# Attention and an ELU network on one core: the next block's operands made at other places of the order, and the weights' sums begun a block earlier

## The chip, the core and the metric

The kernel runs on one core of a Trainium2 chip. The time is the device's, in microseconds (us), of one execution. TensorE (PE) multiplies matrices into PSUM, VectorE (DVE) and ScalarE (ACT) work on PSUM and SBUF, GpSimd (POOL) on SBUF; SyncE (SP) issues all the DMAs of this kernel, in its own order. An engine takes its instructions in order and waits at the first whose inputs or buffer aren't ready.

## The reference

```python
scores = scale * np.matmul(q_c, k_c.transpose(0, 1, 2, 4, 3))   # chunks of 64 positions
scores = scores - np.max(scores, axis=-1, keepdims=True)
attn = np.exp(scores)
attn = attn / (np.sum(attn, axis=-1, keepdims=True) + 1e-09)
out = np.matmul(attn, v_c)
...
x = np.ascontiguousarray(attn_out.transpose(0, 2, 1, 3)).reshape(B * S, H * D)   # 4608 x 512
h = x @ w_in                                                    # 512 -> 2048
g = np.where(h > 0.0, h, alpha * (np.exp(np.minimum(h, 0.0)) - 1.0))
return (g @ w_out).astype(np.float32)                           # 2048 -> 512
```

Batch, heads, positions and head size are 8, 8, 576 and 64. The weights come as doubles (two 32-bit words each).

## The kernel before

A float32 factor is kept as a high part (rounded to the format fp32r) and a low part (the rest), and a product is three matmuls (`three`, L406): high by high, high by low, low by high.

The 4608 rows of x are done in nine blocks of 512, each of four tiles of 128 rows. A tile's attention runs beside the products of the block before: loads of q, k and v; 32x32 transposes on DVE (L283 for q, L286 for k into `k_apart`); scores on PE (L357); softmax (L363 and L377 on DVE, the exponent L381 on ACT, L383 to L385 and the scaling L316 on DVE); eight small DMAs that move rows (y<-y, L328) and a transpose into `a_apart` (L333); the product with v (L341); and a copy into `xf` (L392 on ACT). `k_apart` and `a_apart` exist once, so tiles follow each other in turn.

Blocks 0 and 1 are plain: 16 steps f, each with a product h = x w_in of 128 columns (`hidden`), the ELU (Relu and exponent on ACT L423 and L424, a DVE step L426, a high part ghi on ACT L431, a low part glo on DVE L434), and the product with w_out (`project`). In block 0 the weights are also split into high and low parts (units of `split_units`; L160 is a low part).

Blocks 2 to 8 work in pairs of steps, by Strassen's scheme with seven products of half size instead of eight. Products p1 to p7 need sums of weight quarters (A11 to S4) and of x's quarters (B11, B21, B22 and T1 to T4). p2, p5 and p3 go to one PSUM buffer (y), the rest to another (x). ACT keeps what is in x by copies (c1 to c4, L613), DVE adds y and a kept part (d1 to d3, L618). The results are the halves A (straight) and B (cross) of the pair; each passes through an ELU (L622 and L623 on ACT, L625 on DVE, the high part L630 on ACT, the low part L632 on POOL), and their products with w_out (Q, one per tile of rows) fill PE between the next pair's products.

The weights' sums are made in block 1 by `combine`: for each of eight pairs six operations on POOL (L481, 512 and 256 wide), a copy of 1024 elements to the high part on ACT (L506), the subtract for the low part on POOL (L481, 1024 wide), and DMAs to `a_dram` (L498, L499 for the weights' own parts, L511 for the sums). From there four DMAs for each pair (`load_operands`, L530) bring the operands back, three pairs' places in turn. x's operands are made by `prepare_x` at the end of each block from block 1: differences t1 to t4 on DVE (L554), and for each operand a high part on ACT and a low part on POOL (L558, L559).

PE, ACT, DVE and SP run in the order in which the program is written. That order is set by strings: one item is one step of a generator. H is `hidden`, e a part of an ELU, P a plain step's `project`, a and n steps of the current and the next attention tile, L the next tile's loads, x a step of `prepare_x`, w one load of operands, A and B parts of the two ELUs. LAST_STEP is the last step of block 1, FIRST_PAIR the first pair of block 2, LAST_PAIR a block's last pair. POOL gets its order from the order in which the program names its work.

## Time and profile before

| | |
|---|---|
| median of 3 runs | 908.12 us (906.46 to 908.53) |
| profiled execution | 905.94 us, its span 904.1 us |
| PE busy | 874.0 us (97%) |
| DVE, ACT, POOL busy | 537.4, 497.3, 285.4 us |
| PE clock granted | 0.996 of full |
| DMA | 195.05 MB, 216 GB/s on average |

The span is the time that the records of the profile cover. Block 0 runs up to about 134 us of it, block 1 to about 240, and each of the seven later blocks takes some 94.7 us. "A <- B" in a row is an output and its inputs; in brackets at the end stands how long the engine idled before it and what ended that. Operands of the weights and of the paired ELU's results lie in the memory of the plain weights, so their names read `wi_hi`, `wi_lo`; `h` is PSUM of the first product, `o` of the second, and `t` are the differences.

### The profile page before, as it was taken

How to read it: one execution, taken by the hardware profiler on the slowest of the kernel's cores; microseconds unless marked ns; L12 is line 12 of the kernel's file. 1: busy time of each engine (PE TensorE's matmuls, PEld its weight loads, DVE VectorE, ACT ScalarE, POOL GpSimd, SP SyncE). 2: the span in 40 equal slices, each digit the busy share in tenths (PEclk: the TensorE clock that was granted, in tenths of full speed). 3: DMA queues.
4: the chain of work that ended last, by engine and by line, in shares of the span. 5: the costliest groups of instructions: out<-in, count | busy, mean ns of one | idle time of the engine just before them, and what ended most of it. 6: DMA issues, size and time to landing. Idle time of an engine off the chain costs nothing.

```text
span 904.1 us, 15897 instructions
## 1 busy us (share of the span) xinstructions
PE 874.0 (97%) x5870; PEld 752.6 (83%) x5870; DVE 537.4 (59%) x833; ACT 497.3 (55%) x966; POOL 285.4 (32%) x229
## 2 busy tenths in 40 slices
PE   7899999998989999999999999999999999999998
PEld 6688877876788888888888888887888788889896
DVE  5899888564755576556655665557555755442222
ACT  6899974443444455444644464455444554464443
POOL 2000025677322243224422252226222622253222
PEclk9999999999999999999999999999999999999999
DMA  8785444769887768777679859776768597466421
GB/s 204 214 264 183 161 117 157 241 211 311 248 227 234 240 217 281 233 232 227 202 240 271 253 198 279 227 218 194 260 207 267 166 304 212 177 228 229 166 83 46
DMA packets 161309, 195.05 MB, mean 216 GB/s; under 512 B 67536, under 2 KB 123856, under 8 KB 161232
## 3 DMA queue, kind: packets, MB, share of 16 engines
q1 hardware_dynamic: 161232, 194.04, 68.6%
q8 instruction: 46, 0.75, 0.4%
q14 instruction: 31, 0.25, 0.1%
HBM read 162.53 MB, written 24.12 MB: 206 GB/s over the span
## 4 chain that ended last, share of the span: by engine, by line
PE 73%; DVE 7%; ACT 5%; issue 4%; DMA 4%; POOL 3%; SPq 3%; POOLq 0%; ACTq 0%; DVEq 0%
PE o L406 34%; PE h L406 32%; PE ps_a L357 3%; PE ps_a L341 2%; POOL st L481 2%; DMA wi_hi<-a_dram 1%; DVE t L554 1%; DVE y L316 1%; DMA q_sb<-in_q_dram 1%; SPq L247 1%; POOL wi_lo L632 1%; ACT wi_hi L630 1%; DMA wi_lo<-a_dram 1%; DVE z L383 1%; PE ps_a L265 1%
## 5 line engine op out<-in xcount | busy, mean ns | idle before, releaser
L632 POOL TENSOR_TENSOR wi_lo<-e,wi_hi 128x512 fp32r<-128x512 f32 x112 | 144.9, 1294 | 418.2 <-ACT wi_hi L630 418.2
L613 ACT COPY kept<-h 128x256 f32<-128x256 f32 x224 | 82.1, 367 | 189.8 <-PE h L406 189.7
L618 DVE TENSOR_TENSOR kept<-h,kept 128x256 f32<-128x256 f32 x168 | 70.9, 422 | 191.9 <-PE h L406 133.1
L406 PE MATMUL h<-xhi,wi_hi 128*128 128x256 f32 (+1 forms) x720 | 182.5, 305 | 1.9 <-ACT xhi L558 1.3
L406 PE MATMUL o<-wo_lo,wi_hi 128*128 128x512 f32 x448 | 177.6, 397 | 0.0
L406 PE MATMUL o<-wo_hi,wi_hi 128*128 128x512 f32 x448 | 177.4, 396 | 0.0
L406 PE MATMUL o<-wo_hi,wi_lo 128*128 128x512 f32 x448 | 175.2, 391 | 2.0 <-POOL wi_lo L632 1.6
L406 PEld LDWEIGHTS h<-xhi,wi_hi 128*128 128x128 f32 x720 | 125.3, 189 | 19.7 <-issue 3.2
L406 PE MATMUL h<-xlo,wi_hi 128*128 128x256 f32 (+1 forms) x424 | 133.7, 315 | 2.0 <-DVE xlo L399 1.1
L406 PE MATMUL h<-xhi,wi_lo 128*128 128x256 f32 (+1 forms) x432 | 118.1, 318 | 0.4 <-DVE kept L618 0.4
L406 PEld LDWEIGHTS h<-wi_lo,wi_hi 128*128 128x128 f32 x666 | 94.0, 189 | 14.8 <-ACT kept L613 3.6
L406 PEld LDWEIGHTS o<-wo_hi,wi_lo 128*128 128x128 f32 x448 | 84.2, 188 | 23.8 <-POOL wi_lo L632 5.2
L625 DVE SCALAR_TENSOR_TENSOR e<-e,kept 128x512 f32<-128x512 f32 x112 | 77.3, 690 | 43.5 <-ACT e L623 39.9
L622 ACT ACTIVATE e<-kept 128x512 f32<-128x512 f32 x112 | 70.8, 632 | 55.8 <-DVE kept L618 53.6
L406 PE MATMUL h<-wi_lo,wi_hi 128*128 128x256 f32 x666 | 97.8, 282 | 3.4 <-ACT kept L613 1.7
L630 ACT CAST wi_hi<-e 128x512 fp32r<-128x512 f32 x112 | 69.7, 623 | 47.0 <-DVE e L625 46.6
L406 PEld LDWEIGHTS h<-xlo,wi_hi 128*128 128x128 f32 x424 | 80.0, 189 | 12.7 <-DVE xlo L399 1.8
L406 PEld LDWEIGHTS o<-wo_lo,wi_hi 128*128 128x128 f32 x448 | 85.6, 191 | 2.6
L406 PEld LDWEIGHTS o<-wo_hi,wi_hi 128*128 128x128 f32 x448 | 84.6, 189 | 2.9
L406 PEld LDWEIGHTS h<-xhi,wi_lo 128*128 128x128 f32 x432 | 76.4, 189 | 11.8 <-DVE kept L618 1.6
L623 ACT ACTIVATE e<-e 128x512 f32<-128x512 f32 x112 | 70.8, 632 | 3.6
L481 POOL TENSOR_TENSOR st<-wi_hi,wi_lo 128x512 f32<-128x512 f32 x16 | 22.3, 1418 | 133.0 <-DMA st<-in_k_dram 121.2
(90 smaller groups left out, 1362.0 us busy)
## 6 DMA issues: line engine op xcount, KB each, us to landing
wi_hi<-a_dram SPq DMA_DIRECT2D x148, 448.0 KB, 5.5
wi_lo<-a_dram SPq DMA_DIRECT2D x76, 448.0 KB, 5.3
kept<-in_q_dram SPq DMA_DIRECT2D x80, 128.0 KB, 7.9
kept<-in_k_dram SPq DMA_DIRECT2D x80, 128.0 KB, 5.7
st<-in_moe_w_in_dram SPq DMA_DIRECT2D x16, 512.0 KB, 4.2
st<-in_moe_w_out_dram SPq DMA_DIRECT2D x16, 512.0 KB, 4.7
a_dram<-st SPq DMA_DIRECT2D x16, 512.0 KB, 5.2
y<-y SPq DMA_DIRECT2D x224, 32.0 KB, 1.9
```

What stands on the lines that cost most here:

```text
L247: nc.sync.dma_start(out=qk[p0:p0 + n // U, w0:w0 + NK * U * D].rearrange("p (h w) -> p h w", h=NK), in_=src[b, j::2, s0:s0 + n, :].rearran ...
L341: nc.tensor.matmul(x_ps[j * D:(j + 1) * D, hp, :], lhsT=v_sb[:, h, :], rhs=a_apart[:, h, :], start=True, stop=True,)
L357: nc.tensor.matmul(s_ps[cs, 2 * hp:2 * hp + 2, :], lhsT=qT[:, hp, cs], rhs=kbd[:, hp, :, cs], start=True, stop=True,)
L406: nc.tensor.matmul(ps, lhsT=a, rhs=b, start=start, stop=stop, skip_group_check=onto)
L481: nc.gpsimd.tensor_tensor(out=out, in0=a, in1=b, op=op)
L613: nc.scalar.copy(out=out, in_=self.x)
L618: nc.vector.tensor_tensor(out=out, in0=self.y, in1=self.kept[kept], op=ALU.add)
L622: nc.scalar.activation(out=e, in_=c, func=AF.Relu, scale=-1.0)
L623: nc.scalar.activation(out=e, in_=e, func=AF.Exp, scale=-1.0)
L625: nc.vector.scalar_tensor_tensor(out=e, in0=e, scalar=-1.0, in1=c, op0=ALU.add, op1=ALU.max)
L630: nc.scalar.copy(out=ghi, in_=e)
L632: nc.gpsimd.tensor_tensor(out=glo, in0=e, in1=ghi.bitcast(F32), op=ALU.subtract)
```

## The change

1. **x's operands.** In the order strings the x steps stand at other places, and `prepare_x` goes B11, B21, then the differences t1, t2, t4, then T2, the difference t3, T1, T3, T4, B22 (before: B11, differences, B21, T2, T1, t3 with T3, T4, B22). t1 and t3 take buffers of the plain ELU (`ghi`, `glo` of the pool gp), which the first copies of outputs use too, in place of `y` and `q_sb`. In FIRST_PAIR the projections (Q) stand at other places as well.
2. **The weights' sums.** The three buffers `kept_st` are made at the end of block 0. Sums take the second and third in turn. Those of pairs 0 and 1 are called for in block 0 (f=14 and 15). The low part's subtract moves from POOL to DVE. The stores of the weights' own parts are divided (high or low).
3. **q and k in a buffer of their own.** The tiles of block 1 and the first of the next put q and k all in `kept_st[0]`, each after the one before has been transposed; the last unit of weights is staged in `a_apart`, which is set to zero only afterwards, at the end of block 0.
4. **Loads.** `load_operands` becomes one generator over all pairs; in block 1 two loads of the second pair come earlier than before, and PAIRS has one w more.
5. The last pair's low parts are made on DVE instead of POOL.

The three places at which the prediction rests, in the order of one engine. All line numbers of the changed kernel are shifted (L554 is now L569, L618 L634, L625 L641, L632 L649, L559 L574).

DVE at a block's last pair, the first one, before; `t` are the differences, the two kinds of `kept` the additions d and the ELU's STT:

```order
L618 TENSOR_TENSOR kept<-h,kept 128x256
L554 TENSOR_TENSOR t<-xf 128x512
L554 TENSOR_TENSOR t<-xf,t 128x512 x2
L618 TENSOR_TENSOR kept<-h,kept 128x256
L625 SCALAR_TENSOR_TENSOR e<-e,kept 128x512
L363 TENSOR_REDUCE mx<-ps_a 128x8
L377 TENSOR_TENSOR a<-ps_a,mx 128x512
L383 TENSOR_REDUCE z<-a 128x8
```

And with the change:

```order
L641 SCALAR_TENSOR_TENSOR e<-e,kept 128x512
L367 TENSOR_REDUCE mx<-ps_a 128x8
L381 TENSOR_TENSOR a<-ps_a,mx 128x512
L569 TENSOR_TENSOR t<-xf 128x512
L569 TENSOR_TENSOR t<-xf,t 128x512 x2
L634 TENSOR_TENSOR kept<-h,kept 128x256
L387 TENSOR_REDUCE z<-a 128x8
```

The three differences went from ahead of d1 to behind the first half of the softmax, just ahead of d2.

DVE at the end of block 1 (LAST_STEP) and in the first pair, before; L426 and L434 are the last plain ELU:

```order
L363 TENSOR_REDUCE mx<-ps_a 128x8
L377 TENSOR_TENSOR a<-ps_a,mx 128x512
L554 TENSOR_TENSOR t<-xf 128x512
L554 TENSOR_TENSOR t<-xf,t 128x512 x2
L426 SCALAR_TENSOR_TENSOR e<-e,h 128x512
L434 TENSOR_TENSOR glo<-e,ghi 128x512
L618 TENSOR_TENSOR kept<-h,kept 128x256
L383 TENSOR_REDUCE z<-a 128x8
```

And with the change:

```order
L381 TENSOR_TENSOR a<-ps_a,mx 128x512
L387 TENSOR_REDUCE z<-a 128x8
L388 TENSOR_SCALAR z<-z 128x8
L389 RECIPROCAL z<-z 128x8
L320 TENSOR_TENSOR y<-a,z 128x8x2x32
L569 TENSOR_TENSOR t<-xf 128x512
L569 TENSOR_TENSOR t<-xf,t 128x512 x2
L569 TENSOR_TENSOR t<-xf 128x512
L430 SCALAR_TENSOR_TENSOR e<-e,h 128x512
L438 TENSOR_TENSOR glo<-e,ghi 128x512
```

The rest of the softmax with the scaling, and t3, now stand ahead of the last plain ELU.

SP at the beginning of block 1, before; `st` takes q and k of a tile, in two buffers in turn:

```order
L247 DMA st<-in_q_dram 32x4x256 x4
L247 DMA st<-in_k_dram 32x4x256 x4
L219 DMA v_sb<-in_v_dram 128x8x64
L455 DMA out_dram<-k_sb 128x512
```

And with the change, from the second tile's loads (into the buffer that the first tile's are read from):

```order
L251 DMA kept<-in_q_dram 32x4x256 x4
L251 DMA kept<-in_k_dram 32x4x256 x4
L223 DMA v_sb<-in_v_dram 128x8x64
L459 DMA out_dram<-k_sb 128x512
L459 DMA out_dram<-q_sb 128x512
L459 DMA out_dram<-k_sb 128x512
L459 DMA out_dram<-q_sb 128x512
L519 DMA a_dram<-kept 128x1024 x2
L332 DMA y<-y 32x256 x8
```

The store of the first sums (L519) and the first y moves stand behind loads that wait for the tokens' one buffer.

```diff
@@ -112,8 +112,12 @@
-        st = stp.tile([P, STAGE], U32, name="st")[:, :2 * 4 * P * 2].rearrange(
-            "p (i a b t) -> p i a b t", i=2, a=4, t=2)
+        if u < NF:
+            st = stp.tile([P, STAGE], U32, name="st")[:, :2 * 4 * P * 2]
+        else:
+            st = a_apart.rearrange("p h t -> p (h t)").bitcast(U32)
+        st = st.rearrange("p (i a b t) -> p i a b t", a=4, b=P, t=2)
@@ -480,10 +484,12 @@
+        def place_of(g):
+            return kept_st[1 + g % 2][:, :2 * 8 * P].rearrange("p (l a f) -> p l a f", l=2, f=P)
         def sums(g):
-            st = stp.tile([P, STAGE], F32R, name="st")[:, :2 * 8 * P].rearrange(
-                "p (l a f) -> p l a f", l=2, f=P)
-            w, s = st[:, 0].bitcast(F32), st[:, 1].bitcast(F32)
+            st = place_of(g)
+            w, s = st[:, 0], st[:, 1]
             for i in range(2):
@@ -493,42 +499,51 @@
-            for lo in range(2):
-                w1, w2 = w_in_slices(2 * g)[lo], w_in_slices(2 * g + 1)[lo]
-                nc.sync.dma_start(out=rows(g, lo)[:, :4], in_=w1.bitcast(F32))
-                nc.sync.dma_start(out=rows(g, lo)[:, 4:6], in_=w2[:, 2:].bitcast(F32))
-            return st
...
-        def split(g, st):
-            nc.scalar.copy(out=st[:, 0], in_=st[:, 1].bitcast(F32))
-            pool(st[:, 1], st[:, 1].bitcast(F32), st[:, 0].bitcast(F32), ALU.subtract)
-        def write(g, st):
+        def write_parts(g, lo):
+            w1, w2 = w_in_slices(2 * g)[lo], w_in_slices(2 * g + 1)[lo]
+            nc.sync.dma_start(out=rows(g, lo)[:, :4], in_=w1.bitcast(F32))
+            nc.sync.dma_start(out=rows(g, lo)[:, 4:6], in_=w2[:, 2:].bitcast(F32))
+        def split(g):
+            st = place_of(g)
+            nc.scalar.copy(out=st[:, 0].bitcast(F32R), in_=st[:, 1])
+            nc.vector.tensor_tensor(
+                out=st[:, 1].bitcast(F32R), in0=st[:, 1], in1=st[:, 0], op=ALU.subtract)
+        def write_sums(g):
             for lo in range(2):
-                nc.sync.dma_start(out=rows(g, lo)[:, 6:], in_=st[:, lo].bitcast(F32))
-        made = {}
-        for third in range(3 * NG + 6):
-            g, part = divmod(third, 3)
-            if part == 0 and g < NG:
-                made[g] = sums(g)
-            elif part == 2 and g < NG:
-                split(g, made[g])
-            elif part == 1 and 0 <= g - 1 < NG:
-                write(g - 1, made[g - 1])
-            yield
...
+                nc.sync.dma_start(out=rows(g, lo)[:, 6:], in_=place_of(g)[:, lo])
+        for step in range(-2, NF):
+            for g in range(NG):
+                since = step - (2 * g - 3 if g > 1 else g - 2)
+                if since == 0:
+                    sums(g)
+                    write_parts(g, 0)
+                if since == 1:
+                    split(g)
+                if since == 1 + g % 2:
+                    write_parts(g, 1)
+                if since == 2:
+                    write_sums(g)
+            yield
+    def load_operands():
+        for g in range((NB - PLAIN) * NG):
+            buf, src = place(g % 3), a_dram[g % NG]
+            for i in range(4):
+                part = slice(i * HALF // 2, (i + 1) * HALF // 2)
+                while g > pairs_begun + 1:
+                    yield
+                nc.sync.dma_start(out=buf[:, part].bitcast(F32), in_=src[:, part])
+                yield
@@ -563,19 +578,20 @@
         split("B11", b11, nc.gpsimd)
         yield
-        t1, t2, t4 = t_tile(wst, "y"), t_tile(io, "q_sb"), t_tile(io, "q_sb")
+        split("B21", b21, nc.gpsimd)
+        yield
+        t1, t2, t4 = t_tile(gp, "ghi"), t_tile(io, "q_sb"), t_tile(io, "q_sb")
         minus(t1, b12, b11)
         minus(t2, b22, t1)
         minus(t4, b21, t2)
         yield
-        split("B21", b21, nc.gpsimd)
-        yield
         split("T2", t2, nc.gpsimd)
         yield
+        t3 = t_tile(gp, "glo")
+        minus(t3, b22, b12)
+        yield
         split("T1", t1, nc.gpsimd)
         yield
-        t3 = t_tile(io, "q_sb")
-        minus(t3, b22, b12)
         split("T3", t3, nc.gpsimd)
         yield
         split("T4", t4, nc.gpsimd)
@@ -629,7 +645,8 @@
             ghi, glo = g_places(which)
             nc.scalar.copy(out=ghi, in_=e)
             yield
-            nc.gpsimd.tensor_tensor(out=glo, in0=e, in1=ghi.bitcast(F32), op=ALU.subtract)
+            engine = nc.vector if self.g == (NB - PLAIN) * NG - 1 else nc.gpsimd
+            engine.tensor_tensor(out=glo, in0=e, in1=ghi.bitcast(F32), op=ALU.subtract)
@@ -698,17 +715,18 @@
     PAIRS = (
-        "p1 c1 Q p2 d1 w x B Q x p6 c2 B Q B p5 w n n Q p7 c3 d2 A w a Q Q p4 c4 A w Q p3 d3 A A Q B",
-        "n a a L p1 c1 Q p2 d1 w B Q p6 c2 B Q B n n p5 w Q n p7 c3 d2 A n Q Q p4 c4 A w Q p3 d3 A A "
+        "p1 c1 x Q p2 d1 w B Q p6 c2 B x Q B p5 w x n n Q p7 c3 d2 A w a Q Q p4 c4 A w Q p3 d3 A A "
+        "Q B",
+        "n a a L p1 c1 Q p2 d1 w B Q p6 c2 B Q B n n p5 w Q n p7 c3 d2 A w n Q Q p4 c4 A w Q p3 d3 A A "
         "Q B w",
     )
     LAST_PAIR = (
-        "n a a L p1 c1 x x Q p2 d1 w B Q B x p6 c2 B Q n n x p5 w x Q n p7 c3 d2 A n Q Q p4 c4 x A w "
-        "Q p3 d3 A A Q B w"
+        "n a a L p1 c1 x Q p2 d1 w B Q p6 c2 B Q B x n p5 w x n Q p7 c3 d2 A n Q Q p4 x c4 A w x n Q "
+        "p3 d3 A A x Q B w"
     )
-    LAST_STEP = "n a a n H n x x x P e x e e x e"
+    LAST_STEP = "n a a n H n x x n x P n e x x e e x e"
     FIRST_PAIR = (
-        "p1 c1 p2 d1 w a a Q p6 c2 Q x p5 w x n n Q p7 c3 d2 w A Q a x p4 c4 A w p3 d3 A A B"
+        "p1 c1 x p2 d1 w Q Q x p6 c2 w Q p5 x w p7 c3 Q d2 n n A w p4 c4 A w a p3 d3 A A B"
     )
@@ -773,8 +791,15 @@
-    loads, combining, preparing, pair, kept_st = {}, combine(), iter(()), None, []
+    combining, loading, pairs_begun = combine(), load_operands(), 0
+    preparing, pair, kept_st = iter(()), None, []
...
+    def plain_loads(f: int):
+        for _ in range({LOADED + 1: 1, LOADED + 2: 2, LOADED + 3: 1, NF - 1: 2}.get(f, 0)):
+            next(loading)
+        next(combining, None)
@@ -785,16 +810,17 @@
+    def place_of_tokens(n: int):
+        return kept_st[1 if n % 2 and n > (PLAIN + 1) * NTT else 0]
     def later_loads(n: int):
-        qk = kept_st[n % 2] if kept_st else stp.tile([P, STAGE], F32, name="st")
-        return load_tokens(n * P, qk), load_heads(v, "v_sb", n * P, io)
+        return load_tokens(n * P, place_of_tokens(n)), load_heads(v, "v_sb", n * P, io)
...
     nc.gpsimd.memset(k_apart, 0.0)
-    nc.gpsimd.memset(a_apart, 0.0)
@@ -822,6 +848,10 @@
                     if item == "H":
                         if blk == 0:
                             split_upto(f)
+                            if f == NF - 2:
+                                kept_st += [stp.tile([P, STAGE], F32, name="kept", tag="st")
+                                            for _ in range(3)]
+                                sums = kept_st[2]
                             if f == NF - 1:
                                 loaded = later_loads(2 * NTT)
@@ -848,24 +878,21 @@
+                if blk == PLAIN - 2 and f >= NF - 2:
+                    next(combining)
+                if (blk, f) == (0, NF - 1):
+                    split_upto(NU - 1)
+                    nc.gpsimd.memset(a_apart, 0.0)
                 if blk == PLAIN - 1:
-                    for _ in range(2):
-                        next(combining, None)
-                    if f == NF - 2:
-                        kept_st += [
-                            stp.tile([P, STAGE], F32, name="kept", tag="st") for _ in range(3)]
-                        sums = kept_st[2]
-                        upcoming = later_tile(n + 1, *later_loads(n + 1))
-                    if f >= LOADED:
-                        i = f - LOADED
-                        if i % 4 == 0:
-                            loads[i // 4] = load_operands(i // 4)
-                        next(loads[i // 4])
+                    plain_loads(f)
+                if (blk, f) == (PLAIN - 1, NF - 4):
+                    loaded = load_tokens((n + 1) * P, place_of_tokens(n + 1))
+                if (blk, f) == (PLAIN - 1, NF - 2):
+                    upcoming = later_tile(n + 1, loaded, load_heads(v, "v_sb", (n + 1) * P, io))
...
                 g = (blk - PLAIN) * NG + f // 2
...
-                if g + 2 < (NB - PLAIN) * NG:
-                    loads[g + 2] = load_operands(g + 2)
+                pairs_begun = g + 1
@@ -907,7 +934,7 @@
                     elif item == "w":
-                        next(loads.get(g + 2, iter(())), None)
+                        next(loading, None)
```

7 lines of the change are left out of this document (1 added, 6 removed).

## The prediction

> **What bounds the kernel now.** I read the page first, then busy times by stretch, PE's waits, and the timelines of the places that the change touches.
>
> ```profile
> PE 874.0 (97%) x5870; PEld 752.6 (83%) x5870; DVE 537.4 (59%) x833; ACT 497.3 (55%) x966; POOL 285.4 (32%) x229
> PE 73%; DVE 7%; ACT 5%; issue 4%; DMA 4%; POOL 3%; SPq 3%; POOLq 0%; ACTq 0%; DVEq 0%
> ```
>
> PE is busy for 97% of the span and holds 73% of the chain. The change adds and removes no matmul (in the first pair some only trade places), so what can move are PE's stalls, some 30 us of 904.1. The stretches tell where they lie (length, then PE, PEld, DVE, ACT and POOL busy, PE's clock, DMA):
>
> ```profile
> 135.00:165.00 30.00, 28.27 (x156) 22.81 (x157) 23.40 (x34) 11.70 (x19) 16.32 (x14) 1.00 0.56 192
> 195.00:225.00 30.00, 25.64 (x131) 19.54 (x130) 15.68 (x21) 10.78 (x17) 19.75 (x16) 1.00 0.87 284
> 245.00:257.00 12.00, 8.42 (x62) 7.11 (x63) 6.16 (x9) 6.14 (x13) 5.07 (x4) 0.86 0.78 264
> 395.24:418.41 23.17, 23.17 (x168) 20.65 (x166) 12.48 (x21) 11.21 (x23) 5.18 (x5) 1.00 0.77 227
> 418.41:443.55 25.14, 24.26 (x168) 20.27 (x166) 18.48 (x26) 14.88 (x31) 14.81 (x12) 1.00 0.61 169
> ```
>
> The last two rows run from one tile's value product (L341) to the next. With the same 168 matmuls the one inside a block takes 23.17 and the one over a block boundary 25.14: a stall of 1.97 where POOL works 14.81 instead of 5.18. Five boundaries have such a tile behind them. Block 1 shows 1.73 and 4.36 of idle PE in the first two rows, the handover to the paired work 3.58 in the third.
>
> **Part 1, the end of block 0.** The sums of the first two weight pairs start on POOL when the buffer each takes is free: after the last read of its staging by DVE, which I place at about 109 and 122 from the order of units.
>
> ```profile
> 122.40 0.69 DVE L292 TENSOR_TENSOR a<-a,z 128x512 f32<-128x512 f32 x1
> 123.91 0.60 PE L296 MATMUL ps_a<-ident,a 128*128 128x128 f32 x4
> 127.83 3.29 POOL L481 TENSOR_TENSOR st<-wi_hi,wi_lo 128x512 f32<-128x512 f32 x2 [121.20 <-DMA st<-in_k_dram]
> 128.38 1.61 DVE L160 TENSOR_TENSOR wo_lo<-y,wo_hi 128x512 fp32r<-128x512 f32 x1
> 126.40 0.69 DVE L160 TENSOR_TENSOR wo_lo<-y,wo_hi 128x512 fp32r<-128x512 f32 x1
> 135.08 0.50 PE L406 MATMUL h<-xlo,wi_hi 128*128 128x512 f32 x1 [0.83 <-DVE xlo L399]
> ```
>
> L160 lasts 1.61 where it meets L481 and 0.69 where it doesn't: each holds the other up. Now L481 runs at 122 to 128, and L292 is what it meets. It would end near 125.6 instead of 123.1; its reader L296, at 123.91, is then late by about 1.8, and a glo behind it by 0.3. In return the stall ahead of 135.08 (0.99 by matmul starts, 0.83 by the wait) goes, as POOL is done. Together +1.1; bounds −1 (nothing meets) and +2.1 (the old stall stays).
>
> **Part 2, block 1.** The weights' sums on POOL, their subtracts (L481 with 1024), and what waited for them:
>
> ```profile
> L481 POOL TENSOR_TENSOR st<-st 128x1024 fp32r<-128x1024 f32 x8 | 19.1, 2395 | 15.2 <-ACT st L506 15.2
> 139.94 2.53 POOL L481 TENSOR_TENSOR st<-wi_hi,wi_lo 128x512 f32<-128x512 f32 x2 [5.46 <-DVE k_apart L286]
> 216.38 3.38 POOL L481 TENSOR_TENSOR st<-st 128x256 f32<-128x256 f32 x4
> 219.79 1.05 ACT L506 CAST st<-st 128x1024 fp32r<-128x1024 f32 x1 [5.37 <-POOL st L481]
> 223.42 0.50 PE L406 MATMUL o<-wo_hi,ghi 128*128 128x512 f32 x1 [2.93 <-ACT ghi L431]
> 204.00 1.09 PE L357 MATMUL ps_a<-k_apart,qT 128*64 128x128 f32 x16 [1.31 <-DVE k_apart L286]
> 232.05 1.09 PE L357 MATMUL ps_a<-k_apart,qT 128*64 128x128 f32 x16
> ```
>
> Each sum's subtract (2.4 us on POOL) becomes a DVE instruction of 1024 elements. No such DVE subtract is in this trace. The nearest rows are L160's: two of 512 elements take 1.4, and meeting POOL adds 0.92 (1.61 less 0.69) for each, 3.2. I take 1.4, since few of POOL's operations are left to meet. DVE has room: 15.68 of 30 busy.
>
> POOL ends the last sums at 219.76, ACT stands 5.37 for them at L506, the ELU behind it is late, and PE loses 3.1 (by matmul starts; 2.93 of it is the wait). With eight subtracts off POOL and two sums made before, the sums are not late here: 3.1 goes, a few tenths near 214 too, and of 1.31 at tile 11 about 1.1. Against this, q and k of all tiles of this block go to one buffer. In SP's order tile 9's eight loads stand ahead of the stores of the first block's output, of the sums' stores (now L519) and of the y moves; they wait until tile 8's transposes have read the buffer, which was at 139.9 (the releaser of POOL's row) and is near 142 with the y moves' turn. I get, in order: tile 8's scores +0.85, tile 8's values and the first output +0.2 together, and the third hidden product +2.4, because the sums of pair 2 wait for the store of pair 0's, which is behind SP's wait, and ACT stands at the copy of these sums ahead of an ELU. Parts 1 and 2 so far are 1.1 + 3.45 = 4.6 up to tile 10; from there −1.1 and −3.6 (3.1 and the tenths near 214): tile 11's scores come at 207.5 (204.00 before) and tile 12's at 231.95. Parts 1 and 2 together: −0.15. Bounds: −3 if the early waits hide, and +3 if the late ones stay in part.
>
> **Part 3, the handover.** The rows of that place:
>
> ```profile
> L383 DVE TENSOR_REDUCE z<-a 128x8 f32<-128x512 f32 x32 | 21.9, 684 | 17.0 <-ACT a L381 17.0
> 235.41 1.42 DVE L554 TENSOR_TENSOR t<-xf,t 128x512 f32<-128x512 f32 x2
> 238.81 0.69 DVE L426 SCALAR_TENSOR_TENSOR e<-e,h 128x512 f32<-128x512 f32 x1 [1.98 <-ACT e L424]
> PE h L406 <- ACT xhi L558: 1.3, 1, 1.3
> PE h L406 <- POOL wi_lo L559: 1.0, 1, 1.0
> PE h L406 <- POOL xlo L559: 1.0, 1, 1.0
> PE h L406 <- ACT wi_lo L558: 0.7, 1, 0.7
> 255.41 0.58 PE L406 MATMUL h<-xhi,wi_lo 128*128 128x256 f32 x1
> 242.75 0.69 DVE L316 TENSOR_TENSOR y<-a,z 128x512 f32<-128x512 f32 x1
> ```
>
> Ahead of the last ELU of block 1, DVE now does the normalisation of tile 12 (L383 to L316), the three differences and t3; before, it did only the three. Ahead of L426 stand a reduce of 0.68, two small ones (0.4 together), L316 and t3 (0.69 each): 2.5, and POOL's subtracts of B11 and B21 meet two of them at 0.8 each (1.50 less 0.69, a row of part 4); 1.98 of idle would pay for some, but z must first wait for the exponent behind L392 on ACT. L426 then ends near 242.5 (before 239.5), the second product waits for its PSUM bank and the ELU's products for ghi: 2.3. POOL makes T1 before T2, so p6 is 1.6 late, and ACT's copy of o waits for the buffer that t3 holds, so p7 is 0.8 late. In return the four waits of the list (4.0, all between 244 and 251, for T2, T3, T4 and B22) shrink by some 3.8, as these operands are begun earlier. Tile 13's transposes now stand behind both o copies, so its scores and the value product are 1.0 to 1.9 late. That makes 2.3 + 1.6 + 0.8 − 3.8 + 1.0 (to 1.9) = +1.9 to +2.8 at the end of that value product, 255.41 before. I take the low end, +1.9, because the buffer waits are the steps that I can place least; bounds 0 and +3.
>
> **Part 4, five boundaries.** The rows of that place:
>
> ```profile
> 420.85 2.39 DVE L554 TENSOR_TENSOR t<-xf,t 128x512 f32<-128x512 f32 x2
> 424.96 1.28 POOL L632 TENSOR_TENSOR wi_lo<-e,wi_hi 128x512 fp32r<-128x512 f32 x1 [2.27 <-ACT wi_hi L630]
> 426.20 1.30 POOL L559 TENSOR_TENSOR xlo<-xf,xhi 128x512 fp32r<-128x512 f32 x1
> 427.80 1.50 DVE L316 TENSOR_TENSOR y<-a,z 128x512 f32<-128x512 f32 x1
> 429.55 1.43 DVE L554 TENSOR_TENSOR t<-xf 128x512 f32<-128x512 f32 x1
> 425.73 0.98 PE L406 MATMUL h<-wi_lo,wi_hi 128*128 128x256 f32 x6 [0.42 <-ACT kept L613]
> 429.68 0.39 PE L406 MATMUL h<-xhi,wi_hi 128*128 128x256 f32 x1 [0.17 <-DVE kept L618]
> ```
>
> On DVE the three differences move from before L363/L377 to after them; T1 and T3 separate. Before, 420.85 to 423.24 on DVE delays the tile's softmax; behind its exponent on ACT the keep L613 comes late, and with it the matmuls of 425.73. That goes. But the differences now meet POOL's B glo and B21: starting at 424.07, where L377 ends once they are out of its way, and alternating with rows of 1.28 and 1.30 on POOL, the first ends at 424.76, the second at 426.45, the third at 428.15, and d2 (L618) at 428.5, where its product would allow 426.46. On ACT the ELU of A waits for d2 and the fourth keep (c4) stands behind it, so the next pair's p1 loses 0.7; t3 meets POOL again and d3 makes the next p2 0.5 late, c1 the next p6 0.2: 1.4 in place of 1.97, a gain of 0.57, of which I take 0.45 because of small waits left out. Five times: −2.3. Bounds per boundary: −1.97 (nothing meets) and +0.55 (below).
>
> POOL's 1.43 for a DVE subtract of 0.69 is a wait for the rest of a POOL instruction. [...]
>
> **Part 5, the last boundary and the end.** PE's waits there:
>
> ```profile
> 803.51 0.98 PE L406 MATMUL h<-wi_lo,wi_hi 128*128 128x256 f32 x6 [0.42 <-ACT kept L613]
> 811.65 0.50 PE L406 MATMUL o<-wo_hi,wi_lo 128*128 128x512 f32 x1 [0.37 <-DMA wi_hi<-a_dram]
> wi_hi<-a_dram SPq DMA_DIRECT2D x148, 448.0 KB, 5.5
> 897.76 0.50 PE L406 MATMUL o<-wo_hi,wi_lo 128*128 128x512 f32 x1 [0.16 <-POOL wi_lo L632]
> ```
>
> The last block has no tile after it; its differences then meet nothing on DVE, and what this boundary costs now goes: 0.58 by matmul starts at 803.5 (a keep) and 0.54 at 811.7 (a load of operands, which the added `w` issues earlier). −1.1, bounds −1.1 and 0. At the end the last glo moves to DVE, 0.69 for 1.28, and the stall before 897.76 (0.32 by matmul starts) goes: −0.3. Two loads and a `w` that move earlier on SP, and unit 16's stage in a_apart, I cost at nothing: SP has time between loads in these stretches (DMA share 0.56 to 0.87); without that cover a load of 5.5 us landing late would cost up to as much once.
>
> **Sum:** −0.15 + 1.9 − 2.3 − 1.1 − 0.3 = −1.95 on the span of 904.1, giving 902.2. The profiled execution took 905.94 as a whole, so 904.0; the median of the runs shown, 908.12, lies 2.18 above it, so **906.2 us**.
>
> **The rivals.** *Clean boundaries:* the differences miss POOL, so 1.97 goes whole: 5 × (1.97 − 0.45) = 7.6 more, 898.6. For it: L377 and the differences are short, and 0.1 us decides who starts first. Against it: B's glo and B21 are ready on POOL in just these 2 us. *Block 1 runs at PE's pace:* SP's wait hides and tile 12 comes at 229, −2.85 more, 903.3. For it: PE has 28.27 of 30 in 135:165 now; against it: the wait at the single buffer is real in SP's order. *SP's queue decides (slower):* what I charged once, 2.4 for a store of sums behind loads that wait for a buffer, comes again at tiles 10 and 11, +4.8: 911.0. It does so once a tile's transposes start later than the next sums are wanted. Against it: later loads stand behind the y moves, which are spread over 25 us. *The boundaries get worse (slower):* if the three differences each wait for a whole POOL instruction, d2 ends 1.1 later than I have it (two waits of 1.30 instead of 0.74) and a boundary costs 2.5, 0.55 more than now: 5 × (0.55 + 0.45) = 5.0 more, 911.2. It decides as soon as d2 ends after 429.6, where it ends now (its reader starts at 429.68). For and against it: the rows above, of 1.43 against 1.30 + 0.69. That only the order changes and nothing comes of it lies within the forecast's spread.
>
> **How the numbers follow.** Forecast 0.38, clean boundaries 0.13, block 1 at PE's pace 0.20, SP's queue 0.17, worse boundaries 0.12. A change under 0.2% (1.8 us) can't be told from none here: faster is under 906.3, slower above 909.9. The forecast lies at the edge, with a spread of about 2 from its bounds: 0.19 faster, 0.16 same, 0.03 slower. The second gives 0.13 faster; the third 0.17 faster, 0.03 same; the two slower ones 0.06 same and 0.23 slower. Sums: faster 0.49, same 0.25, slower 0.26. The range of 8 in 10 runs from 900.5, short of the clean case, to 911.3; the forecast's own is 903.5 to 909.
>
> **What would show it.** Right: a boundary interval of 24.5 to 24.9 instead of 25.14, with L554 longer than 1 us; tile 12's scores near 232; no ACT stand of 5 us at L506's successor near 219; a stall of 2 near 241. Wrong: the interval at 23.2 or above 25.2, tile 12 before 230 or after 234, or the end of that value product back at 255.

## The result: 0.9% slower, and the profile after

The changed kernel takes 916.77 us (median of 7 runs, 911.30 to 919.10) against 908.22 (7 runs, 906.46 to 910.23): a ratio of 1.009 with the 95% interval 1.0065 to 1.0115. The forecast was 906.2, with a range up to 911.3. The profiled execution after took 919.10, the longest of its runs, with a span of 917.3; so stages are compared by the intervals between the starts of the tiles' scores (the score product is now L361, the value product L345), which leave the start of the run out. Block 0 makes tiles 4 to 7, block 1 tiles 8 to 11 with tile 12, and so on.

| us | tile 6 to 7 | 7 to 8 | 8 to 12 | 12 to 14 (handover) | over a boundary | tile 35 to the last matmul |
|---|---|---|---|---|---|---|
| before | 25.70 | 23.20 | 91.53 | 44.45 | 25.14 | 126.96 |
| after | 27.28 | 25.80 | 94.77 | 49.67 | 25.36 | 125.12 |

Parts 1 and 2 of the forecast (−0.15) became 1.58 + 2.60 + 3.24 = +7.4, part 3 (+1.9) became +5.2, part 4 (−2.3) became 5 × 0.22 = +1.1, part 5 (−1.4) became −1.8. That is 11.9 in this execution; the medians differ by 8.55. Part of the difference is PE's clock: within the handover it was granted at half for 10.2 us here and for 3.4 before, and other runs with the same handover take as little as 47.4 us for it (experiment 4).

The page, and stretches of the profile after (columns as before). Tiles 7 to 8, 9 to 10 and 12 to 13 are cut at the scores; the last two rows, one interval inside a block and one over a boundary, at the value products. Each cut lies 0.13 to 0.14 ahead of the first matmul:

```profile
PE 877.3 (96%) x5870; PEld 754.4 (82%) x5870; DVE 558.5 (61%) x843; ACT 498.3 (54%) x966; POOL 273.1 (30%) x219
120.07:145.87 25.80, 23.00 (x136) 17.56 (x136) 23.69 (x31) 17.00 (x42) 7.63 (x7) 1.00 0.34 91
160.44:188.45 28.01, 25.09 (x128) 19.47 (x128) 19.33 (x23) 10.21 (x16) 14.37 (x14) 1.00 0.67 215
240.64:263.97 23.33, 17.84 (x110) 14.96 (x110) 15.25 (x21) 10.93 (x21) 8.89 (x7) 0.93 0.73 230
409.28:432.45 23.17, 23.17 (x168) 20.65 (x166) 12.48 (x21) 11.21 (x23) 5.18 (x5) 1.00 0.74 230
432.45:457.80 25.35, 24.23 (x168) 20.33 (x166) 18.59 (x26) 15.16 (x31) 15.45 (x12) 1.00 0.58 180
```

DVE is the engine that got busier (558.5 for 537.4), and it is 92% and 69% busy in the first two stretches. PE's waits after, largest of this middle part:

```profile
PE ps_a L361 <- DVE k_apart L290: 8.2, 6, 2.2
PE h L410 <- DVE e L430: 2.6, 1, 2.6
PE ps_a L300 <- ACT e L427: 2.1, 1, 2.1
PE ps_a L361 <- ACT k_apart L281: 1.4, 1, 1.4
```

The wait for ACT's ghi behind POOL's sums (2.93) is gone, as forecast. In its place PE waits 8.2 us in all for tiles' transposes.

### The profile page after: what moved, and what is told of

The parts are those of the page before. It is cut to its first block, busy times and chain, and to the rows that moved or that the text cites. A ratio compares the mean times of both kernels' runs of the same rounds, so it can differ in the third digit from the quotient of the medians.

```text
span 917.3 us, 15884 instructions
## 1 busy us (share of the span) xinstructions
PE 877.3 (96%) x5870; PEld 754.4 (82%) x5870; DVE 558.5 (61%) x843; ACT 498.3 (54%) x966; POOL 273.1 (30%) x219
## 5 line engine op out<-in xcount | busy, mean ns | idle before, releaser
L649 POOL TENSOR_TENSOR wi_lo<-e,wi_hi 128x512 fp32r<-128x512 f32 x110 | 145.3, 1321 | 400.5 <-ACT wi_hi L646 400.5
L634 DVE TENSOR_TENSOR kept<-h,kept 128x256 f32<-128x256 f32 x168 | 71.0, 423 | 210.8 <-PE h L410 155.7
L641 DVE SCALAR_TENSOR_TENSOR e<-e,kept 128x512 f32<-128x512 f32 x112 | 78.8, 704 | 43.9 <-ACT e L639 41.1
L485 POOL TENSOR_TENSOR kept<-wi_hi,wi_lo 128x512 f32<-128x512 f32 x16 | 24.6, 1561 | 163.5 <-DVE y L185 111.1
```

What stands on the lines that cost most here:

```text
L485: nc.gpsimd.tensor_tensor(out=out, in0=a, in1=b, op=op)
L634: nc.vector.tensor_tensor(out=out, in0=self.y, in1=self.kept[kept], op=ALU.add)
L641: nc.vector.scalar_tensor_tensor(out=e, in0=e, scalar=-1.0, in1=c, op0=ALU.add, op1=ALU.max)
L649: engine.tensor_tensor(out=glo, in0=e, in1=ghi.bitcast(F32), op=ALU.subtract)
```

## The experiments

Two times are given: the run's median, and the median of the kernel before in the same set.

**1. The subtract of the sums: undone, done alone, and moved.** `a_split_pool` is the changed kernel with

```diff
-            nc.vector.tensor_tensor(
-                out=st[:, 1].bitcast(F32R), in0=st[:, 1], in1=st[:, 0], op=ALU.subtract)
+            pool(st[:, 1].bitcast(F32R), st[:, 1], st[:, 0], ALU.subtract)
```

> The changed kernel with the subtract of the weights' sums back on POOL. Theory that the subtract on DVE (1.2 to 2.35 us in the changed kernel, ahead of the softmax's first step) lengthens the loop of block 1: the intervals between tiles 9 and 12 fall by 1 to 2 each, the time by 2 to 5. Rival, that POOL is too slow for the sums again, as before the change: ACT stands at the copy of sums and the time stays or rises by up to 3.

909.53 against 907.65, ratio 1.0029 (1.0012 to 1.0045): of the 0.9% two thirds are gone. The intervals of tiles 8 to 12 fall from 14.58, 28.01, 26.26 and 25.92 to 12.13, 24.98, 24.54 and 25.54, together by 7.6; in neither of the two profiles is PE at half clock there.

`b_split_dve` is the kernel before with `pool(...)` in `split` made `nc.vector.tensor_tensor(...)`.

> The kernel before with one edit: the subtract of the weights' sums moves from POOL to DVE. Theory that this is the largest single cause, since DVE stands in the loop that paces block 1: block 1 (scores of tile 7 to tile 12) takes 118 to 121 us instead of 114.7, the time rises by 3 to 6, 911 to 914. Rival, that the subtract only hurts together with the tokens' one buffer and the sums in block 0: block 1 gets shorter, since the stall of 3.1 behind POOL's last sums goes, and the time falls by 1 to 3.

913.59 against 908.83, ratio 1.0059 (1.0041 to 1.0076). Tiles 7 to 12 take 121.1 instead of 114.7, and 1.7 of it is a stretch at half clock. So it needs neither the one buffer of the tokens nor the early sums. Its waits in block 1:

```profile
PE ps_a L357 <- DVE k_apart L286: 6.8, 4, 2.0
PE o L406 <- ACT ghi L431: 3.1, 2, 2.4
```

`a_split_late` leaves the subtracts on DVE, but calls that of a third step (f = 4k + 2) after the next tile's first softmax steps instead of before them:

```diff
+                    if blk == PLAIN - 1 and st == 3 and at_item == 4:
+                        plain_loads(f - 1)
...
-                if blk == PLAIN - 1:
+                if blk == PLAIN - 1 and st != 2:
                     plain_loads(f)
```

> The changed kernel with three of DVE's subtracts (those that stand just ahead of the softmax's first steps of tiles 9, 10 and 11) moved behind these steps, with the ACT copies ahead of them. DVE does the same work. Theory that the place on DVE decides, as each subtract of 1.4 to 2.35 us stands in the loop: the intervals from tile 9 to 12 fall by 1.5 to 2 each, the time by 3 to 5, 912 to 914. Rival, that DVE's amount of work or its meeting POOL decides: within 1.5 of the changed kernel.

913.30 against 908.83, ratio 1.0046 (1.0030 to 1.0062): the intervals of tiles 9 to 12 are 24.57, 25.08 and 24.62, together 74.3 and 5.9 less, with the same work on DVE. Two more runs that keep the changed kernel's order here, `a_sums_swap` and `a_trio_late`, take 79.6 and 78.9, so 4.6 to 5.9 is the gain. So it is the place of this step: the subtract with ACT's copy ahead of it, and what SP issues in the step moves along. In the timelines, DVE, SP and PE of the changed kernel between tiles 10 and 11:

```profile
189.84 0.69 DVE L438 TENSOR_TENSOR glo<-e,ghi 128x512 fp32r<-128x512 f32 x1 [0.69 <-ACT ghi L435]
190.79 2.35 DVE L514 TENSOR_TENSOR kept<-kept 128x1024 fp32r<-128x1024 f32 x1 [0.25 <-ACT kept L513]
193.07 0.68 DVE L367 TENSOR_REDUCE mx<-ps_a 128x8 f32<-128x512 f32 x1
200.58 1.06 DVE L320 TENSOR_TENSOR y<-a,z 128x512 f32<-128x512 f32 x1
201.66 5.18 SPq L332 DMA_DIRECT2D y<-y  x8
206.89 2.00 SPq L251 DMA_DIRECT2D kept<-in_q_dram  x4
208.94 1.85 SPq L251 DMA_DIRECT2D kept<-in_k_dram  x4
211.38 1.10 DVE L287 STREAM_TRANSPOSE qT<-kept 128x512 f32<-128x512 f32 x1 [0.42 <-DMA kept<-in_q_dram]
212.50 2.21 DVE L290 STREAM_TRANSPOSE k_apart<-kept 64x512 f32<-64x512 f32 x2
214.85 1.09 PE L361 MATMUL ps_a<-k_apart,qT 128*64 128x128 f32 x16 [1.25 <-DVE k_apart L290]
```

and the same place with the subtract moved (tile 10's scores start at 187.05 here, 188.59 above):

```profile
188.92 0.68 DVE L367 TENSOR_REDUCE mx<-ps_a 128x8 f32<-128x512 f32 x1
190.62 2.22 DVE L514 TENSOR_TENSOR kept<-kept 128x1024 fp32r<-128x1024 f32 x1 [0.29 <-ACT kept L513]
```

This is a loop: scores, first softmax step, scaling (L320), y moves (5.2 us on SP), the next tile's loads behind them, transposes, scores. It has no slack that DVE's idle time would fill: from the start of tile 10's scores to L367 are 4.5 us in the one and 1.9 in the other, and the next scores follow 26.3 and 25.1 after.

**2. The loop's other part.** `a_loads_first` issues the next tile's loads ahead of the y moves:

```diff
+                if early:
+                    following = later_tile(n, *later_loads(n))
                 if blk == 1:
                     next(tile_now, None)
                     next(tile_now, None)
```

> The changed kernel, but in block 1 the loads of the next tile's q, k and v are issued ahead of the current tile's eight y moves instead of behind them (tiles 10 to 12). Theory that block 1 runs at the pace of one loop (scores, softmax, scaling, y moves, the next loads, transposes, scores): the moves' 5 us leave the loop, the intervals between tiles 9 and 12 fall from 28.0, 26.3 and 25.9 to about 24, the time by 5 to 8 us, to 909 to 912. Rival, that DVE's own work sets the pace: intervals stay above 25.5 and the time falls by less than 1.5.

913.37 against 907.65 (1.0064, 1.0049 to 1.0079). The intervals of tiles 9 to 12 fall by 1.8, 2.4 and 0.9 to 26.18, 23.88 and 24.97: less than the 5 us that left the loop. In DVE's order a_apart's transposes, which wait for the moves (1.8 us between tiles 10 and 11), stand ahead of k_apart's; that this is the next limit is likely, but was not tested. The time, expected at 909 to 912, doesn't stand clear of the changed kernel's. The same edit on the kernel before, with the low parts of the last pair on DVE, `b_loads_end`:

> The kernel before with two edits: in block 1 the next tile's loads ahead of the y moves, and the last pair's low parts on DVE. Theory of the loop: the intervals of 25.2 and 25.5 between tiles 9, 10 and 11 fall to about 24, that of 28.05 stays above 26 because ACT stands at the copy of the last sums, and the end gives 0.3: the time 2 to 4 under before, 904 to 906. Rival, that the loop is not the limit in this kernel: only the 0.3 shows.

908.77 against 908.53, 1.0010 (0.9996 to 1.0024). One interval fell (25.50 to 23.88), the ones around it rose (25.21 to 26.50 and 28.05 to 30.15). In the last, 1.6 of the rise is a stretch at half clock. The stand of ACT at the copy of POOL's last sums, which was expected to keep this interval long, is gone; instead the ELU's step on DVE stands behind a_apart's transposes, which wait for the y moves:

```profile
226.42 0.70 DVE L333 STREAM_TRANSPOSE a_apart<-y 64x512 f32<-64x512 f32 x1 [5.30 <-DMA y<-y]
228.60 0.69 DVE L426 SCALAR_TENSOR_TENSOR e<-e,h 128x512 f32<-128x512 f32 x1
229.99 0.80 PE L406 MATMUL o<-wo_hi,ghi 128*128 128x512 f32 x1 [3.27 <-ACT ghi L431]
```

A shorter loop gives nothing where the next wait takes it back.

**3. Block 0.** `a_unit16` stages the last unit of weights in the ring again (the edit of `load_unit` undone).

> The changed kernel with the last unit of weights staged in the ring of three buffers as before, not in a_apart; so the sums' buffers come free one unit later each, and the first sums start near 125 instead of 110.7. Theory that the sums on POOL at 110 to 120 double DVE's operations in block 0 and delay the ELU, k_apart and the scores of tile 7: the interval between the scores of tiles 6 and 7 goes from 27.3 to 25.7, the time by 1 to 2, near 915. Rival, that what is won there is lost by tile 9 (later sums, later stores): time within 0.7 of the changed kernel.

913.97 against 908.53 (1.0067, 1.0049 to 1.0084); the interval of tiles 6 to 7 is 25.70 again, and that of 7 to 8 stays at 25.78. The first sums start at 115.4 there, not near 125. The time alone doesn't stand clear of the changed kernel's; the interval does. POOL, DVE and ACT of the changed kernel there:

```profile
110.65 3.32 POOL L485 TENSOR_TENSOR kept<-wi_hi,wi_lo 128x512 f32<-128x512 f32 x2 [104.92 <-DVE y L185]
111.03 1.78 DVE L438 TENSOR_TENSOR glo<-e,ghi 128x512 fp32r<-128x512 f32 x1
112.74 2.31 DVE L179 SCALAR_TENSOR_TENSOR y<-st 128x1024 uint32<-128x1024 uint32 x1
117.97 0.63 ACT L435 CAST ghi<-e 128x512 fp32r<-128x512 f32 x1 [2.99 <-DVE e L430]
```

DVE's 1.22 and 0.69 become 2.31 and 1.78, ACT waits 3 us for the ELU's step, and makes `k_apart` of tile 7 behind it. `a_sums_swap` was to delay the first sums by exchanging their two buffers (`kept_st[2 - g % 2]`); tile 13's q and k then come down over the last pair's sums, so that pair's values differ while the instructions are the same.

> The changed kernel with the two buffers of the sums exchanged, so that the first sums wait for the later of two staging buffers and start near 126 instead of 110.7. Theory that the sums on POOL at 110.7 to 119.7 delay DVE in block 0: the interval between the scores of tiles 6 and 7 falls from 27.3 to 25.7 and the time by 1 to 2. Rival, that block 1's loop starts when its first sums are stored: what is won at tile 7 is lost by tile 9, and the time is within 1 of the changed kernel or above it.

915.16 against 907.65 (1.0085). POOL started at 110.3 as before, so the run tells nothing of the question. Perhaps its order took whichever sums have the buffer that is free first; the trace doesn't show which sums came first.

**4. x's preparation.** `a_old_x` takes part 1 of the change back whole (strings, order, buffers); `b_new_x` does it alone.

> The changed kernel with x's preparation (order of its steps, their places in the order strings, the two buffers) as it was before; the sums, the tokens' buffer, the loads and the end stay changed. The changed kernel's profile loses 5.2 us at the handover (tile 12's scores to tile 14's: 49.7 us instead of 44.4) and 0.22 at each of five boundaries. Theory that each part costs where it stands: the handover is back near 44.5, the boundary interval at 25.14 instead of 25.36, the time 6 us under the changed kernel, near 910.5. Rival, that the handover is late because tile 12 comes late out of block 1: only the 1.1 of the boundaries comes back, 915.5.

914.27 against 907.65 (1.0076, 1.0054 to 1.0099). Handover 46.82, boundary 25.13. Six more runs with the changed handover (`a_split_pool`, `a_split_late`, `a_loads_first`, `a_unit16`, `a_sums_swap`, `a_trio_late`) take 47.38 to 49.50 for it, so 0.6 to 2.9 came back: neither the theory nor the rival. A late tile 12 is not needed for the rest: `c_best` and `c_two` (below) have the old preparation and a shorter block 1 than before (tiles 9 to 12 in 74.8 and 76.7, 78.8 before), and still take 46.01 and 47.30. In all three, PE has a wait of 1.4 to 1.8 in the handover ahead of the first one of before. Which part of the change brings it stays open.

> The kernel before, with the new preparation of x alone (its steps' order, their places in the strings, the two buffers, the places of Q in the first pair). Theory that this part costs where it stands, as the changed kernel against the one with x as before shows (49.7 against 46.8 us from tile 12's scores to tile 14's, 25.36 against 25.14 at a boundary): handover 47 to 48 instead of 44.45, boundaries 25.36, the time 2.5 to 4 above before, 910.2 to 911.7. Rival, that it only costs where tile 12 comes late out of block 1, which it does not here: handover under 45, time within 1.5 of before. The forecast on record for this part was +1.9 at the handover and -2.3 at the boundaries.

911.61 against 908.53 (1.0038, 1.0023 to 1.0053). Handover 47.68, boundary 25.34, from tile 35 to the end 125.64 (126.96 before). So with this part alone the handover is 3.2 longer. Of these, 1.8 lie ahead of tile 13's scores. The other 1.4 lie behind them, where PE waits no longer than before but runs at half clock for 6.1 us instead of 3.4. In the changed kernel's profile the two are 2.96 and 2.26, the second with 6.8 us at half clock and 0.9 of idle. In all seven runs with the changed handover tile 13's scores come 23.3 after tile 12's (20.4 before), while from tile 13 to 14 it takes 24.1 to 26.3 (24.1 before). So about 3 us come with the change each time, and up to 2.3 more mostly with the clock.

`a_trio_late` moves one item in the changed kernel's LAST_PAIR:

```diff
-... p5 w x n Q p7 c3 d2 A n Q Q p4 x ...
+... p5 w n Q p7 c3 d2 x A n Q Q p4 x ...
```

> The changed kernel with one item of one string moved: the three differences behind d2 in a block's last pair. Theory that they, held by POOL, hold d2: the boundary interval falls from 25.36 to 24.92, as in the faster kernel, five times 0.43, and the time by about 2. Rival, that the lower interval there comes from something else that the faster kernel has not changed (splits on POOL, loads): 25.3 stays.

The boundary takes 24.93. In time it doesn't stand out (915.05 against 909.39, 1.0067), since block 1 scatters by more. At a boundary of the changed kernel:

```profile
438.36 1.30 POOL L649 TENSOR_TENSOR wi_lo<-e,wi_hi 128x512 fp32r<-128x512 f32 x1 [1.52 <-ACT wi_hi L646]
438.63 1.58 DVE L569 TENSOR_TENSOR t<-xf 128x512 f32<-128x512 f32 x1
440.24 2.39 DVE L569 TENSOR_TENSOR t<-xf,t 128x512 f32<-128x512 f32 x2
442.55 0.42 DVE L634 TENSOR_TENSOR kept<-h,kept 128x256 f32<-128x256 f32 x1
445.19 0.38 PE L410 MATMUL h<-xhi,wi_lo 128*128 128x256 f32 x1 [0.50 <-ACT kept L629]
445.25 1.78 DVE L569 TENSOR_TENSOR t<-xf 128x512 f32<-128x512 f32 x1
447.42 0.39 PE L410 MATMUL h<-xhi,wi_lo 128*128 128x256 f32 x1 [0.55 <-DVE kept L634]
```

and in a kernel with the differences behind d2:

```profile
431.33 0.42 DVE L642 TENSOR_TENSOR kept<-h,kept 128x256 f32<-128x256 f32 x1 [1.90 <-ACT kept L637]
431.67 0.68 DVE L554 TENSOR_TENSOR t<-xf 128x512 f32<-128x512 f32 x1
432.39 1.42 DVE L554 TENSOR_TENSOR t<-xf,t 128x512 f32<-128x512 f32 x2
```

There d2 waits for its input and the differences run at 0.68 and 0.71 each, after POOL has done its two.

**5. Versions that beat both.** `c_best` and `c_two` undo several parts together:

> The changed kernel with four parts undone or altered together: x's preparation as before, the subtract on POOL, unit 16 in the ring, and the next tile's loads ahead of the y moves; what stays of the change is the early sums, the tokens' buffer, the loads and the low parts of the last pair on DVE. If the gains add (2.5, 7.2, 1.5 and 1 to 3): 903 to 905, under before. If the loop of block 1 is already at PE's pace once the subtract is off DVE, the loads give nothing: 905.5 to 907.

910.59 against 908.53 (1.0027), over both forecasts: the gains don't add. Tiles 7 to 8 take 28.83. Of this 1.7 is half clock, and PE waits 2.8 for the split of x on DVE (four operations of L399 in 5.73 us), beside the first subtract on POOL at 137.75. `a_unit16`, whose sums start as late but whose subtract is on DVE, takes 25.78 there and 3.57 for the four.

> The changed kernel with x's preparation as before, the subtract on POOL, and the next tile's loads ahead of the y moves; unit 16 stays in a_apart (in the kernel that also put it back, the interval from tile 7 to 8 took 28.8 instead of 25.8). Theory that that interval was the cost of the sums starting later: 25.2 from tile 7 to 8 and 27.2 from 6 to 7, block 1 near 112 instead of 115.7, the time 906.5 to 908, like before. Rival, that 28.8 has another cause: 910 again.

911.91 against 908.83 (1.0032): tiles 7 to 8 take 25.11, as the theory had it, but the handover 47.30, with PE at half clock for 10.2 us of it, and the time is nearer the rival's.

`b_trio_late` is the kernel before, with the new order of x's preparation in blocks 2 to 8 only (`prepare_x(late=True)`, the string of `a_trio_late`) and the last pair's low parts on DVE.

> The kernel before with the changed order of x's preparation in blocks 2 to 8 only, but with the three differences behind d2 instead of ahead of it, and the last pair's low parts on DVE. Block 1 and the handover are as before. Theory that at a boundary of the changed kernel d2 waits for differences that wait for POOL: without them ahead of it, the interval falls from 25.36 to 24 to 24.6, under the 25.14 of before; the last boundary and the end give 1.8; the time is 4 to 8 under before, 900.5 to 904.5. Rival, that the stall only moves on, to the operands made from the late differences (T2 for p6): the interval stays at 25.1 to 25.6 and only the 1.8 shows.

905.88 against 908.83, ratio 0.9967 (0.9952 to 0.9983): faster than before. The boundary is 24.92, the end 125.61: a gain of 0.22 for each boundary where 0.5 to 1.1 was expected, and the time misses its range of 900.5 to 904.5. The stall moved in part, as the rival had it, but to d3: PE waits 1.2 for it ahead of the next p2.

`d_hand` adds to it the changed handover, with L426 ahead of tile 12's normalisation (LAST_STEP `n a a n H n x x x P e e n n x x e x e`, FIRST_PAIR as changed).

> The faster kernel of the last set (before, with the differences behind d2 at later boundaries and the end's low parts on DVE), and in it the changed handover, with one difference to the change: the last plain ELU's step on DVE (L426) stands ahead of tile 12's normalisation and scaling again. Theory that the changed handover loses by the 2.4 to 2.8 us for which the second product waits for L426: handover (scores of tile 12 to 14) 45 to 46 instead of 47.7 with the whole new order, 44.45 with the old. Rival, that the later stall decides, 2.3 us ahead of tile 13's scores, whose transposes stand behind both output copies and d2: it stays, and the handover is at 47 to 48 again.

907.39 against 909.39 (0.9983, 0.9968 to 0.9999). Handover 45.32 instead of 47.68: L426's stall is gone, but the low part L434 now stands behind the normalisation and PE waits 2.3 for it, and 2.1 for tile 13's transposes remain. PE's idle time in the handover is no less than in `b_new_x` (5.3 and 4.8); what is less is the time at half clock, 3.4 instead of 10.2. `d_hand2` moves both (LAST_STEP `n a a n H n x x x P e e e x e n n x x`, FIRST_PAIR with `n n` ahead of p5):

> The kernel of d_hand with two more places changed: the last plain ELU's low part (L434) also stands ahead of tile 12's normalisation, and tile 13's transposes stand between the two output copies on DVE instead of behind both. Theory that these are the two stalls that d_hand still shows (2.48 ahead of the first product with glo, 2.30 ahead of tile 13's scores): the handover falls from 45.3 to 41 to 42, under the 44.45 of before; the time is 5 to 6.5 under before, 1.5 to 3 under the faster kernel. Rival, that the stalls pass to x's operands (T2, T1) that come later: handover 43.5 to 45.5.

904.29 against 907.87, ratio 0.9963 (0.9948 to 0.9978), the lowest ratio of all, though its interval overlaps that of `b_trio_late`; handover 44.01, about the old one. So the rival's number was right: the named waits went and others came. They are not the ones it named (T2 and T1), but kept parts, c and d:

```profile
PE h L406 <- ACT kept L637: 2.1, 1, 2.1
PE h L406 <- DVE kept L642: 1.0, 1, 1.0
PE ps_a L341 <- issue: 0.7, 1, 0.7
```

## Why the prediction was wrong

**The step that failed** is in part 2: the subtract on DVE was costed at nothing, "DVE has room: 15.68 of 30 busy". The size was not the failure (1.23 to 2.35, 1.32 in the median, against 1.4 taken), nor the relief of POOL, which came as forecast. But in block 1 DVE stands in a loop that paces PE, and three of the subtracts stood in it between the scores and the first softmax step, with ACT's copy ahead of them. The forecast followed SP's queue and POOL through this block and did not put the subtracts into the tile's own chain; doing this alone costs 0.6%, undoing it brings back two thirds of 0.9%. With the subtract back on POOL the intervals of parts 1 and 2 sum to −0.9 (1.54 + 1.94 − 4.34), not far from the forecast's −0.15; as changed they sum to +7.4, so tile 12's scores come 147.9 after tile 6's instead of 140.3.

**Part 1** foresaw that L292 would be late by meeting the sums (1.8; PE waited 2.1 ahead of L300; the list above puts this down to ACT's L427, which ends last by 0.15, while in `c_two` the same wait is DVE's) and that the old stall of 0.99 would go, which it did. It left out what the first sums at 110 do: the forecast placed them at 109 and followed only those at 122. They cost 1.6 at tile 7, as the run with unit 16 in the ring shows.

**Part 2's wait on SP** is there: tile 9's loads start at 143.9 after tile 8's transposes, the store of the first sums at 150.6, and POOL waits 19.5 for it. What it costs by itself was not taken apart: no run gave the tokens a second buffer.

**Part 3** had the right waits with wrong sizes: 2.3 for L426 (2.4 by matmul starts in the kernel with the new preparation alone, 2.75 in the changed one), 0.8 for p7 (0.53), 1.0 to 1.9 for tile 13's transposes (2.3). The 1.6 for T2 behind T1 did not come here. The four waits that were to shrink by 3.8 are gone. PE's idle time from tile 12 to 14 rose by 2.5 (3.97 to 6.44), near the +1.9 to +2.8 forecast; that it is so near is partly luck, since terms that came larger stand against one that didn't come. The term missing is PE's clock: the prediction's own row for 245 to 257 shows it at 0.86, and it was not followed. At half clock for 10.2 us instead of 3.4, PE lost 4.7 us in the handover instead of 1.7, in part in place of waiting: `a_unit16`, at full clock up to tile 13's scores, has them after the same 23.3 us. DVE and PE of the changed kernel:

```profile
246.90 1.50 DVE L320 TENSOR_TENSOR y<-a,z 128x512 f32<-128x512 f32 x1
250.97 0.68 DVE L430 SCALAR_TENSOR_TENSOR e<-e,h 128x512 f32<-128x512 f32 x1
251.70 0.58 PE L410 MATMUL h<-xhi,wi_hi 128*128 128x256 f32 x1 [2.59 <-DVE e L430]
259.89 0.69 DVE L457 COPY k_sb<-o 128x512 f32<-128x512 f32 x1 [3.50 <-PE o L410]
260.83 1.12 DVE L287 STREAM_TRANSPOSE qT<-kept 128x512 f32<-128x512 f32 x1
264.11 1.09 PE L361 MATMUL ps_a<-k_apart,qT 128*64 128x128 f32 x16 [2.17 <-DVE k_apart L290]
```

**Part 4** had the mechanism: d2 runs from 442.55 to 442.97. The value products of the two boundaries lie 14.17 apart (432.59 and 418.42), so d2 ends at 428.8 in the old count, where 428.5 was forecast. Mis-sized was what follows: 0.66 ahead of the next p1 (forecast 0.7), 0.71 ahead of p2 (0.5), 0.17 ahead of p6 (0.2), and left out 0.23 ahead of p3, and about 0.1 at the first matmul after each of the four stalls. Their sum is 2.2 instead of 1.4, so 1.97 saved became 0.22 lost.

**Part 5** held in sum: −1.8 for −1.4; the new preparation gives 1.3 of it and the low parts 0.5.

**The rivals.** Block 1 at PE's pace, clean boundaries: no. The two slower ones, 911.0 and 911.2, came nearest in time, but not in cause. SP's queue: at tiles 10 and 11 PE waited for DVE's transposes and not for sums. Worse boundaries: right in sign, by 0.22 instead of 0.55; the wait for a whole POOL instruction (1.30) that its sum takes for two of the differences is shown by no run: in the changed kernel the three took 1.58, 1.67 and 0.69 from 438.63 on, so two of them 0.89 and 0.98 longer than 0.69. No rival had the subtract in DVE's loop. Two of the signs of being wrong came, tile 12 after 234 and the interval above 25.2; the stand of ACT near 219 went, as the other list said.

## What to carry to other kernels

Before work is moved to an engine because it is idle half the time, follow the loop that paces the stage through that engine's order and see where the moved instruction lands in it: with the same subtracts behind the softmax's first step three tiles took 4.6 to 5.9 us less than with them ahead of it. Where POOL's TENSOR_TENSORs met DVE's differences, subtracts and scalings here, these took up to 1.1 us longer (a difference 1.67 instead of 0.69, a glo 1.78 instead of 0.69), so such work on POOL belongs where DVE's next instructions have no reader waiting. And gains of single edits did not add here: each removed wait uncovered the next, so measure them together. PE's granted clock was 0.50 for 3.4 us of the handover before and for 10.2 with the change; where a stall comes ahead of such a stretch, count the time at half clock in each profile before a difference of 2 us between two profiles is put down to an edit.

## What the runs showed of the hardware

After a stall of 2.75 us (PE's last matmul at 248.84, the next at 251.70) PE ran at half its clock for about 3.4 us:

```profile
248.80:251.50 2.70, 0.31 (x3) 0.11 (x1) 2.63 (x5) 0.62 (x1) 0.00 (x0) 1.00 1.07 305
252.00:252.50 0.50, 0.50 (x3) 0.50 (x3) 0.12 (x1) 0.50 (x2) 0.00 (x0) 0.50 0.08 23
254.50:255.00 0.50, 0.50 (x3) 0.40 (x2) 0.00 (x0) 0.00 (x0) 0.50 (x1) 0.50 0.09 25
255.50:256.00 0.50, 0.50 (x6) 0.47 (x5) 0.31 (x1) 0.00 (x0) 0.50 (x1) 1.00 0.24 66
```

The column before the last two is the granted clock, 0.50 and then 1.00 again; a 512-wide matmul starts every 0.43 us instead of 0.227. By these figures, an estimate, this stall cost about 1.7 us (half of 3.4) more than its length. A stall of 2.25 at 128.9 in the same execution was not followed by it.

The length of a stall did not decide alone in these runs. The stall of 2.25 was followed by half clock in `a_split_late`, `a_old_x` and `a_trio_late` (from 130.8, 129.2 and 129.8 on). The wait of 2.9 for ghi in block 1 was not in the kernel before and in `d_hand2`, but was in `b_new_x`, `b_trio_late` and `d_hand`. In the changed kernel's trace the stretches at half clock begin at 36.61, 251.65 and 265.31 and last 3.41, 3.41 and 6.83 us; in that of before they begin at 34.69 and 253.14 and last 3.41 each. From one to the next are 63, 4 and 64 times 3.413 us. Counted in steps of that length in these two traces, from 20 us to the last matmul, four steps at full clock had PE busy for under 35%, and each was followed by half clock; of six with 43% to 59% one was, of 501 with more none. That it matters into which steps a stall falls is the author's reading of these counts. Below are the step ahead of the half clock in the changed kernel, the one with the wait for ghi in `b_new_x`, and the larger part of the same wait in the kernel before, where it falls into two steps:

```profile
248.24:251.65 3.41, 0.87 (x7) 0.66 (x5) 3.34 (x6) 0.62 (x1) 0.00 (x0) 1.00 1.05 320
221.98:225.39 3.41, 1.02 (x3) 0.59 (x4) 1.72 (x3) 2.59 (x5) 2.24 (x1) 1.00 0.32 91
219.01:222.42 3.41, 1.48 (x7) 0.90 (x5) 0.39 (x1) 2.17 (x3) 2.24 (x2) 1.00 0.67 254
```

PE was busy for 26%, 30% and 43% of them; only the third was followed by full clock.

DVE's 1024-wide STT of SBUF data took 2.31 instead of 1.22 beside POOL, and a TENSOR_SCALAR 1.22 instead of 0.69 (119.00 in the same execution): not only subtracts of two tensors were held up here. In the traces of before and after, the 40 differences and scalings (L554 and L316, now L569 and L320) that took over 0.9 us instead of 0.69 each ended 0.54 to 0.55 us after the end of a POOL instruction that had begun before them.
